# Attention weights' sums in a 128x12 layout for the reciprocal, result copied out ahead of it, value products in three steps a pair

## The chip, the cores and the metric

The kernel runs on one core of one Trainium2 chip. The metric is the time of one execution on the device in microseconds (us), here the median of three runs of the kernel before. A profile is one further execution, recorded by the hardware profiler. The core's engines are TensorE (PE; its weight loads are listed apart as PEld), VectorE (DVE), ScalarE (ACT), GpSimd (POOL) and SyncE (SP), which issues the DMAs. Each engine works through its own list of instructions in order and waits on semaphores for the others. PE writes only to PSUM, from which DVE and ACT read.

## The reference

Two stages: attention in which a query sees only keys of its own cluster, and a mixture of experts on its result.

```python
B, H, S, D = 4, 8, 768, 64          # 16 clusters, 8 experts, DM = 512, DF = 1024
q_assign = argmax(q_n . c_n); k_assign = argmax(k_n . c_n)
mask = q_assign[..., :, None] == k_assign[..., None, :]
scores = where(mask, scale * q @ k.T, -1e9)
scores = scores - scores.max(-1)
attn = exp(scores)
attn = attn / (attn.sum(-1) + 1e-9)
attn_out = attn @ v                              # (B, H, S, D)

x = attn_out.transpose(0, 2, 1, 3).reshape(B * S, H * D)
P = exp(logits - logits.max())                   # logits = x @ w_gate
for _ in range(8): P is normalized by rows, then by columns
for e in range(E):
    out += P[:, e:e+1] * (relu(x @ w1[e]) @ w2[e])
```

A query whose cluster holds no key has the same score everywhere. Its row of attention is then 1/S for every key; the kernel treats such rows by a flag.

## The kernel before, in words

Attention is done in 16 pairs of heads (4 batches of 8 heads). For a pair, q and k are loaded and transposed on PE, split into a high and a low part, and assigned to clusters. For each head, max_chunk (L673) computes scores on PE and takes row maxima on DVE (L688, L692), max_rows (L698) joins them, transposes them and sends them by DMA into rows of the query operand. exp_chunk (L734) computes the scores again, transposed: keys on the partitions, 512 or 256 queries in the free dimension, nine chunks (CHUNKS, L181), each with two products for a tile (L751, L752), and ACT takes the exponential into a tile "pe" (L758), of which there are 14 (PB). The running sum of pe over the blocks of keys goes into a tile "psum" of 128 by 768 in SBUF, on POOL or DVE (L777).

values(p) (L788) multiplies pe with v for both heads of a pair at once: head 0 goes to partitions 0 to 63 of one PSUM tile av_ps (the only one), head 1 to 64 to 127 (L808), chunk by chunk. A small product adds the mean of v for the flagged rows (L816). Then, for 512 and for 256 queries, PE sums psum over its 128 partitions by a product with ones and spreads the sum over the 64 rows of its head (L830); a product with one5 adds the flag and 1e-9 (L831). DVE takes the reciprocal of the whole 128x512 or 128x256 tile (L836) and multiplies av_ps with it into xT (L839). Only then are the tile av_ps and the sums given back, and values of the next pair is started. release (L781) gives a pe tile back once its product and its sum are done.

All of this is a set of Python generators, and nothing of the order is written out by hand: each says on which engine its next step runs and for how long by its own estimate (`yield PE, 0.87, ...`), and a planner (L59) picks steps by start time and by a key (KEYS, L413; urgency, L421: nine units a head). The order that comes out is fixed for every engine. Tokens stand for buffers, so t_v (1) for av_ps, t_x (2) for the two PSUM tiles misc_ps that all small products share, t_pe for the 14 pe tiles. out_batch (L852) writes a batch's xT to memory and computes its logits (L871).

The experts' stage follows. Its weights are loaded and split into fp16 parts (L1020 to L1042), its products are L1110 in the first layer and L1172 to L1174 in the second. Its SBUF tiles lie where those of attention were.

Of the kernel before, what the change touches and what calls it, by code (L numbers as in the profile page):

```python
# [20 lines left out]
P = 128  # L21
# [131 lines left out]
def attn_moe_kernel(  # L153
# [154 lines left out]
    with ExitStack() as actx:  # L308
# [9 lines left out]
        def misc_tile():  # L318
            return ps_x.tile([P, 512], F32, name="misc_ps")
# [55 lines left out]

        mrs = [sm.tile([P, NT, 3], F32, name=f"mrt{i}", bufs=1) for i in range(4)]

        nhs = [sm.tile([5, S], F32R, name=f"nht{i}", bufs=1) for i in range(3)]
# [4 lines left out]
        for t in nhs:  # L383
            nc.vector.memset(t.bitcast(F32), 1.0)
        row5 = sm.tile([5, 1], F32, name="row5", bufs=1)
        nc.gpsimd.iota(row5, pattern=[[0, 1]], base=0, channel_multiplier=1, allow_small_or_imprecise_dtypes=True)
        up2 = sm.tile([5, 1], F32, name="up2", bufs=1)
        nc.vector.tensor_scalar(out=up2, in0=row5, scalar1=2.0, scalar2=None, op0=ALU.is_ge)
        odd = sm.tile([4, 1], F32, name="odd", bufs=1)
        nc.vector.scalar_tensor_tensor(out=odd, in0=up2[0:4], scalar=-2.0, in1=row5[0:4], op0=ALU.mult, op1=ALU.add)  # L390
# [3 lines left out]
        one5 = sm.tile([5, 2, D], F32R, name="one5", bufs=1)  # L394
        tiny = sm.tile([5, 1], F32, name="tiny", bufs=1)
        nc.vector.tensor_scalar(out=tiny, in0=row5, scalar1=4.0, scalar2=1e-9, op0=ALU.is_equal, op1=ALU.mult)
        for x in range(2):
            c_ = sm.tile([5, 1], F32, name=f"of{x}", bufs=1)
            nc.vector.tensor_scalar(out=c_, in0=up2, scalar1=float(x), scalar2=1.0 / S, op0=ALU.is_equal, op1=ALU.mult)
            for g in range(x, G, 2):  # L400
                nc.vector.tensor_copy(halves[:, g], c_[0:4].broadcast_to([4, D]))
            o_ = sm.tile([5, 1], F32, name=f"on{x}", bufs=1)
            nc.vector.scalar_tensor_tensor(out=o_, in0=row5, scalar=2.0 * x, in1=tiny, op0=ALU.is_equal, op1=ALU.add)
            nc.vector.tensor_copy(one5[:, x], o_.broadcast_to([5, D]))

        free = iter([(last[nm, i], f"{nm}{i}") for nm, i in kept])

# [2 lines left out]
        plan = Planner(tc)  # L410
        plan.free.update({PE: 6.0, ACT: 4.0, DVE: 6.3, POOL: 9.0, SP: 2.0})

        KEYS = dict(load=-20, split0=-98.0, split1=-72.5, split2=-33.5, assign=-29.0, place=-30.0, chain=-27.5, ones=-29, max=-18, rows=-38.0, exp=0, values=13.5, out=12.0, batch=27.0, group=-30.0, vsplit=-17.0, vsum=2.5, group0=-18.5, inputs=8, first=1000)  # L413
        NL = 32
        GATES = [0, 0, 1, 0]
        COSTS = [0.66, 0.46, 0.432, 0.214, 0.42]
# [281 lines left out]
        def max_rows(n):  # L698
            for c in range(NCH):
                yield ev["m", n, c]  # L700
            t = heads[n]
            m_, qa = mm[n % 3], t["qa"]
            yield DVE, 0.081
            mr = sm.tile([P, NT], F32, name="mr1")
            nc.vector.tensor_reduce(out=mr, in_=t["mr"], axis=AX, op=ALU.max)
            yield ACT, 0.19
            nc.scalar.copy(m_[:, 0:NT], mr)
            yield POOL, 0.1
            nc.gpsimd.tensor_scalar(out=m_[:, 2 * NT : 3 * NT], in0=mr, scalar1=-BIG / 2, scalar2=None, op0=ALU.is_le)
# [24 lines left out]
        def exp_chunk(n, c):  # L734
# [36 lines left out]
            for part in parts:  # L771
                if a not in old:
                    old[a] = part
                    continue
                n_ = z - a
                e = yield (POOL, 0.06 + n_ * 0.0023), (DVE, 0.08 + n_ * 0.00104, RELUCT[2])
                (nc.gpsimd if e == POOL else nc.vector).tensor_tensor(out=st[:, a:z], in0=old[a], in1=part, op=ALU.add)  # L777
                old[a] = st[:, a:z]
            ev["s", n, c].set(plan)

        def release(p, c):  # L781

            c2 = c + 1 if c == 0 else c
            for x in range(2):
                yield ev["s", 2 * p + x, c2]
                t_pe.put(plan)

        def values(p):  # L788
# [7 lines left out]
            ve = gr["ve"][:, h % G : h % G + 2].rearrange("p h d -> p (h d)")  # L796
            nh = nhs[p % 3]
            av = None
            for c in range(NCH):
                for x in range(2):  # L800
                    yield ev["p", n + x, c]
                yield PE, 0.87, 0.107, 0.43
                if c == 0:
                    av = ps_v.tile([P, 1024], F32, name="av_ps")
                i0, ni, a, z = CHUNKS[c]
                for i in range(i0, i0 + ni):
                    for t, vn, o in two:
                        nc.tensor.matmul(  # L808
                            av[o, a:z], vn[:, i, :], heads[t]["pe", c][:, i - i0], start=(i == 0), stop=False, skip_group_check=True
                        )  # L810
                plan.spawn(release(p, c), plan.now.key)
            for x in range(2):
                yield ev["nh", n + x]
            yield PE, 0.34, 0.107, 0.11
            for a, z in SPANS:
                nc.tensor.matmul(av[:, a:z], ve, nh[0:4, a:z], start=False, stop=True, skip_group_check=True)  # L816
            if h % G == G - 2:
                t_vn.put(plan)
            if h == 0:
                if b:  # L820
                    yield ev["batch", b - 1]
                xts[b] = sm.tile([P, NC, S], F32, name="xT", bufs=1)
            for x in range(2):
                yield ev["s", n + x, NCH - 1]
            for a, z in SPANS:
                yield t_x
                yield PE, (z - a) * 0.0021, 0.107, 0.11
                ps = misc_tile()
                for t, vn, o in two:
                    nc.tensor.matmul(ps[o, 0 : z - a], ones[:, 0:D], heads[t]["sum"][:, a:z], start=True, stop=False, skip_group_check=True)  # L830
                nc.tensor.matmul(  # L831
                    ps[:, 0 : z - a], one5.rearrange("p x d -> p (x d)"), nh[:, a:z], start=False, stop=True, skip_group_check=True
                )
                yield DVE, 0.08 + (z - a) * 0.00104
                ri = work.tile([P, z - a], F32, name="ri", bufs=2)
                nc.vector.reciprocal(ri, ps[:, 0 : z - a])  # L836
                t_x.put(plan)
                yield DVE, 0.08 + (z - a) * 0.00104
                nc.vector.tensor_tensor(out=xts[b][:, h // 2, a:z], in0=av[:, a:z], in1=ri, op=ALU.mult)  # L839
            for x in range(2):  # L840
                t_nh.put(plan)
                t_sum.put(plan)
                ev["v", n + x].set(plan)
            t_v.put(plan)
            if p + 1 < npairs:
                plan.spawn(values(p + 1), urgency("values", 2 * p + 2))
            if h == H - 2:
                plan.spawn(out_batch(b), urgency("batch", n + 1))

# [67 lines left out]
        for n in range(nheads):  # L917
# [389 lines left out]
```

## Time and profile before

| what | us |
|---|---|
| median of three runs | 2567.76 (2566.76 to 2575.36) |
| the profiled execution | 2566.92 |
| its span, first to last instruction | 2565.1 |
| PE busy in the span | 2438.1 |
| DVE busy | 1401.9 |
| ACT busy | 807.5 |
| POOL busy | 674.8 |
| last write of xT (L839) in attention starts at | 609.3 |

A row of a profile group gives the line, the engine, the operation, output and inputs with their shapes, the count, then the busy time in us, the mean time of one in ns, and the engine's idle time just before them with what ended it. A matmul's time in the trace holds its latency, so that two pipelined ones overlap: their rate is read from one start to the next. An fp32 product is recorded as two instructions. PEclk is the share of PE's clock that was granted.

### The profile page before, as it was taken

The numbers are of one execution on the slowest core, as the hardware profiler recorded it, in microseconds if no ns is written. First come the engines' busy times: TensorE is split into PE (matmuls) and PEld (weight loads), VectorE is DVE, ScalarE is ACT, GpSimd is POOL, SyncE is SP. The second block draws the span as 40 slices with busy tenths as digits, with TensorE's granted clock in tenths as the row PEclk, the third lists the DMA queues.
The fourth block names the chain that finished last, engine by engine and source line by source line (L and its number), as shares of the span: only waits on it lengthen the run. The fifth ranks groups of instructions, "written<-read, shape, count | busy, mean of one in ns | idle before, by whom it ended". The sixth has DMA issues, their size and how long they took to land.

```text
span 2565.1 us, 32392 instructions
## 1 busy us (share of the span) xinstructions
PE 2438.1 (95%) x12720; PEld 1281.4 (50%) x12720; DVE 1401.9 (55%) x2349; ACT 807.5 (31%) x1493; POOL 674.8 (26%) x679
## 2 busy tenths in 40 slices
PE   6999999997888999999999999999999999999999
PEld 3455555443444445455545455555555555555554
DVE  7778778686866554444444445644444343443444
ACT  4344444344424242424242422222212222122221
POOL 5667665674424141505050500000000000000000
PEclk7999998999899999999999999999999999999999
DMA  8444434324776554334342422322223223232232
GB/s 179 114 102 110 82 96 103 100 54 146 263 294 236 198 167 137 128 120 158 110 156 99 147 83 85 140 90 97 107 91 112 92 94 110 91 111 93 92 114 93
DMA packets 154681, 320.28 MB, mean 125 GB/s; under 512 B 61088, under 2 KB 90528, under 8 KB 154016
## 3 DMA queue, kind: packets, MB, share of 16 engines
q1 hardware_dynamic: 154528, 318.21, 39.1%
q8 instruction: 100, 1.64, 0.3%
q14 instruction: 53, 0.43, 0.1%
HBM read 230.74 MB, written 58.72 MB: 113 GB/s over the span
## 4 chain that ended last, share of the span: by engine, by line
PE 76%; DVE 9%; POOL 6%; issue 4%; DMA 3%; ACT 1%; SPq 0%; POOLq 0%; ACTq 0%; DVEq 0%
PE h_ps L1110 28%; PE o_ps L1174 11%; PE o_ps L1172 11%; PE o_ps L1173 11%; PE av_ps L808 5%; PE max_ps L688 3%; PE exp_ps L751 3%; DVE ri L836 2%; PE exp_ps L752 2%; POOL r L1030 2%; DMA r<-in_moe_w 2%; DVE mrt L692 2%; POOL wa L1042 2%; DVE am L286 1%; DMA scan<-in_moe_w 1%
## 5 line engine op out<-in xcount | busy, mean ns | idle before, releaser
L1110 PEld LDWEIGHTS <-wa 128*128 128x128 f16 x5376 | 527.6, 98 | 477.4 <-issue 49.8
L1122 DVE SCALAR_TENSOR_TENSOR hl<-c,hh 128x384 f16<-128x384 f32 x512 | 315.4, 616 | 539.9 <-ACT hh L1121 539.4
L1110 PE MATMUL h_ps<-xsT,wa 128*128 128x384 f16 x3072 | 586.0, 327 | 16.1 <-DVE u L1132 10.4
L1174 PE MATMUL o_ps<-wb,hl 128*128 128x512 f16 x1536 | 583.6, 380 | 4.8 <-DVE hl L1122 4.8
L1172 PE MATMUL o_ps<-wb,hh 128*128 128x512 f16 x1536 | 585.0, 381 | 0.0
L1173 PE MATMUL o_ps<-wb,hh 128*128 128x512 f16 x1536 | 584.4, 380 | 0.0
L1121 ACT ACTIVATE hh<-c 128x384 f16<-128x384 f32 x512 | 266.9, 521 | 844.9 <-DVE c L1132 840.5
L1110 PE MATMUL h_ps<-xsB,wa 128*128 128x384 f16 x2304 | 425.4, 329 | 23.1 <-DVE c L1132 14.5
L777 POOL TENSOR_TENSOR psum<-psum,pe 128x512 f32<-128x512 f32 (+1 forms) x237 | 251.5, 1071 | 123.1 <-ACT pe L758 116.4
L758 ACT ACTIVATE pe<-exp_ps 128x512 f32<-128x512 f32 x288 | 168.1, 596 | 267.5 <-PE exp_ps L752 245.9
L1174 PEld LDWEIGHTS <-hl 128*128 128x128 f16 x1536 | 150.6, 98 | 187.4 <-DVE hl L1122 7.3
L1132 DVE SCALAR_TENSOR_TENSOR c<-h_ps,u 128x384 f32<-128x384 f32 x256 | 142.0, 555 | 180.8 <-PE h_ps L1110 179.6
L692 DVE TENSOR_REDUCE mrt<-max_ps 128x1 f32<-128x512 f32 (+1 forms) x288 | 189.8, 680 | 91.9 <-PE max_ps L688 91.0
L1132 DVE SCALAR_TENSOR_TENSOR u<-h_ps,m 128x384 f32<-128x384 f32 x256 | 141.9, 554 | 158.6 <-PE h_ps L1110 158.6
L1172 PEld LDWEIGHTS <-hh 128*128 128x128 f16 x1536 | 151.0, 98 | 141.6 <-issue 2.6
L1173 PEld LDWEIGHTS <-hh 128*128 128x128 f16 x1536 | 151.0, 98 | 140.5 <-issue 2.6
L1137 ACT ACTIVATE c<-h_ps 128x384 f32<-128x384 f32 x128 | 62.5, 489 | 416.6 <-PE h_ps L1110 416.6
L808 PE MATMUL av_ps<-pe,vn 128*64 128x512 f32 (+1 forms) x768 | 153.0, 510 | 8.8 <-DVE xT L839 8.8
L1034 POOL TENSOR_TENSOR wa<-r,wa 128x256 f16<-128x256 f32 (+1 forms) x62 | 58.8, 967 | 389.6 <-ACT wa L1033 389.6
L688 PE MATMUL max_ps<-kX,qX 96*128 96x256 f32 (+1 forms) x384 | 130.3, 408 | 23.1 <-DVE mrt L692 22.6
L1192 DVE SCALAR_TENSOR_TENSOR acc<-o_ps,gates,acc 128x512 f32<-128x512 f32 x168 | 125.3, 746 | 45.7 <-PE o_ps L1174 45.7
L752 PE MATMUL exp_ps<-qX,kX 98*128 98x256 f32 (+1 forms) x384 | 134.5, 361 | 0.0
(187 smaller groups left out, 1966.7 us busy)
## 6 DMA issues: line engine op xcount, KB each, us to landing
wa<-wd SPq DMA_DIRECT2D x96, 896.0 KB
wb<-wd SPq DMA_DIRECT2D x96, 512.0 KB
r<-in_moe_w SPq DMA_DIRECT2D x64, 512.0 KB
wd<-wa SPq DMA_DIRECT2D x32, 896.0 KB
scan<-in_moe_w SPq DMA_DIRECT2D x56, 512.0 KB
wd<-wb SPq DMA_DIRECT2D x32, 512.0 KB
qn<-in_q SPq DMA_DIRECT2D x16, 384.0 KB
kn<-in_k SPq DMA_DIRECT2D x16, 384.0 KB
```

The source lines that it names most:

```text
L688: nc.tensor.matmul(ps[:, y * (z - a) : (y + 1) * (z - a)], t["qa"][0:96, i * P : (i + 1) * P], t["k2"][0:96, a:z], start=True, stop=True)
L692: nc.vector.tensor_reduce(out=t["mr"][:, i0 : i0 + ni, ni - 1], in_=ps.rearrange("p (x c) -> p x c", x=ni), axis=AX, op=ALU.max)
L752: nc.tensor.matmul(o, t["k2"][0:98, ki], t["qa"][0:98, a:z], start=False, stop=True)
L777: (nc.gpsimd if e == POOL else nc.vector).tensor_tensor(out=st[:, a:z], in0=old[a], in1=part, op=ALU.add)
L808: nc.tensor.matmul(av[o, a:z], vn[:, i, :], heads[t]["pe", c][:, i - i0], start=(i == 0), stop=False, skip_group_check=True)
L1110: nc.tensor.matmul(ps[:, 0:HB], wa[:, w_, a, c, :], x[:, x_, c, :], start=(first and s_ == 0), stop=(s_ == len(steps) - 1), skip_group_che ...
L1121: nc.scalar.activation(hh[:, 2 - i, o], src, AF.Relu)
L1122: nc.vector.scalar_tensor_tensor(out=hl[:, 2 - i, o], in0=src, scalar=0.0, in1=hh[:, 2 - i, o], op0=ALU.max, op1=ALU.subtract)
L1132: nc.vector.scalar_tensor_tensor(out=t, in0=ps[:, 0:HB], scalar=KAPPA, in1=x, op0=ALU.mult, op1=ALU.add)
L1172: nc.tensor.matmul(po[i], hh[:, t, ti], wbh[:, t], start=(first and t == 0), stop=False)
L1173: nc.tensor.matmul(po[i], hh[:, t, ti], wbl[:, t], start=False, stop=False)
L1174: nc.tensor.matmul(po[i], hl[:, t, ti], wbh[:, t], start=False, stop=(last and t == 1))
```

## The change

- Value products: a step of values(p) holds three chunks in place of one, so that a pair has three steps.
- values(p) ends with two copies of av_ps to xT on ACT; then av_ps is free and the next pair's values may start.
- A new generator norm(p) takes over the sums. Four products put the sums of a head's halves in four groups of 32 partitions, ACT copies them, three transposes turn them so that queries lie on the partitions, and DVE adds 1e-9 and the flag, takes the reciprocal and splits it into two fp32r parts, on 128x12 values (2 heads of 6 blocks of 128 queries). One transpose brings them to 24x128, ACT copies, and six products with the constant "spread" put each query's reciprocal on its head's 64 rows. DVE multiplies that into xT.
- The flags come from POOL in max_rows in the 128x6 layout, and are no longer taken from the row that a DMA fills; the row of ones in nhs and the constant one5 go.
- Two keys and three planned costs are changed.

```diff
-        KEYS = dict(..., max=-18, ..., vsum=2.5, ...)
+        KEYS = dict(..., max=-27, ..., vsum=-10, ...)
...
+            if n >= 8:
+                yield ev["norm", n // 2 - 4]
+            yield POOL, 0.1
+            o = n % 2 * NT
+            nc.gpsimd.tensor_scalar(out=flags[n // 2 % 4][:, o : o + NT], in0=mr, scalar1=-BIG / 2, scalar2=None, op0=ALU.is_le)
             yield t_x
             yield PE, 0.063, 0.107, 0.06
...
-                e = yield (POOL, 0.06 + n_ * 0.0023), (DVE, 0.08 + n_ * 0.00104, RELUCT[2])
+                e = yield (POOL, 0.33 + n_ * 0.0019), (DVE, 0.1 + n_ * 0.00125, RELUCT[2])
...
-            for c in range(NCH):
-                for x in range(2):
-                    yield ev["p", n + x, c]
-                yield PE, 0.87, 0.107, 0.43
+            for u in range(NCH // 3):
+                for c in range(3 * u, 3 * u + 3):
+                    for x in range(2):
+                        yield ev["p", n + x, c]
+                yield PE, 2.8, 0.107, 0.43
...
+            for a, z in SPANS:
+                yield ACT, 0.15 + (z - a) * 0.00083
+                nc.scalar.copy(xts[b][:, h // 2, a:z], av[:, a:z])
+            t_v.put(plan)
+            ev["raw_x", p].set(plan)
...
-                for t, vn, o in two:
-                    nc.tensor.matmul(ps[o, 0 : z - a], ones[:, 0:D], heads[t]["sum"][:, a:z], start=True, stop=False, skip_group_check=True)
-                nc.tensor.matmul(
-                    ps[:, 0 : z - a], one5.rearrange("p x d -> p (x d)"), nh[:, a:z], start=False, stop=True, skip_group_check=True
-                )
-                yield DVE, 0.08 + (z - a) * 0.00104
-                ri = work.tile([P, z - a], F32, name="ri", bufs=2)
-                nc.vector.reciprocal(ri, ps[:, 0 : z - a])
-                t_x.put(plan)
-                yield DVE, 0.08 + (z - a) * 0.00104
-                nc.vector.tensor_tensor(out=xts[b][:, h // 2, a:z], in0=av[:, a:z], in1=ri, op=ALU.mult)
...
+        def norm(p):
...
+            for g in range(4):
+                nc.tensor.matmul(
+                    ps[g * Q : (g + 1) * Q, 0:HS], ones[:, 0:Q], heads[n + g // 2]["sum"][:, g % 2 * HS : (g % 2 + 1) * HS], start=True, stop=True
+                )
...
+            nc.scalar.copy(sc, ps[:, 0:HS])
...
+            for j in range(NT // 2):
+                nc.tensor.transpose(out=ps2[:, j * P : (j + 1) * P], in_=sc[:, j * P : (j + 1) * P], identity=ident)
...
+            nc.vector.reciprocal(rs, rs)
...
+            nc.tensor.transpose(out=ps.bitcast(F32R)[0 : 2 * R, 0:P], in_=rr.rearrange("p y r -> p (y r)"), identity=ident_r)
...
+            yield ev["raw_x", p]
+            for a, z in SPANS:
...
+                for i in range(a // P, z // P):
+                    nc.tensor.matmul(
+                        ps[:, i * P - a : (i + 1) * P - a], spread[:, i].rearrange("r x d -> r (x d)"), rt, start=True, stop=True
+                    )
+                yield DVE, 0.15 + (z - a) * 0.00104
+                x_ = xts[b][:, h // 2, a:z]
+                nc.vector.tensor_tensor(out=x_, in0=ps[:, 0 : z - a], in1=x_, op=ALU.mult)
...
+        for p in range(npairs):
+            plan.spawn(norm(p), urgency("out", 2 * p + 1))
```

More of the change, by code (lines that the diff above doesn't have):

```diff
@@ L376, in attn_moe_kernel @@
         mrs = [sm.tile([P, NT, 3], F32, name=f"mrt{i}", bufs=1) for i in range(4)]
-        nhs = [sm.tile([5, S], F32R, name=f"nht{i}", bufs=1) for i in range(3)]
+        nhs = [sm.tile([4, S], F32R, name=f"nht{i}", bufs=1) for i in range(3)]
         for t in mm:
@@ L382, in attn_moe_kernel @@
             nc.vector.memset(t, -BIG / 2)
[L383 to L388, printed above, removed]
+        flags = [sm.tile([P, 2 * NT], F32, name=f"flags{i}", bufs=1) for i in range(4)]
+        row4 = sm.tile([4, 1], F32, name="row4", bufs=1)
+        nc.gpsimd.iota(row4, pattern=[[0, 1]], base=0, channel_multiplier=1, allow_small_or_imprecise_dtypes=True)
+        up2 = sm.tile([4, 1], F32, name="up2", bufs=1)
+        nc.vector.tensor_scalar(out=up2, in0=row4, scalar1=2.0, scalar2=None, op0=ALU.is_ge)
         odd = sm.tile([4, 1], F32, name="odd", bufs=1)
-        nc.vector.scalar_tensor_tensor(out=odd, in0=up2[0:4], scalar=-2.0, in1=row5[0:4], op0=ALU.mult, op1=ALU.add)
+        nc.vector.scalar_tensor_tensor(out=odd, in0=up2, scalar=-2.0, in1=row4, op0=ALU.mult, op1=ALU.add)
         sgn4 = sm.tile([4, 1], F32, name="sgn4", bufs=1)
@@ L411, in attn_moe_kernel @@
         plan.free.update({PE: 6.0, ACT: 4.0, DVE: 6.3, POOL: 9.0, SP: 2.0})
-        KEYS = dict(load=-20, split0=-98.0, split1=-72.5, split2=-33.5, assign=-29.0, place=-30.0, chain=-27.5, ones=-29, max=-18, rows=-38.0, exp=0, values=13.5, out=12.0, batch=27.0, group=-30.0, vsplit=-17.0, vsum=2.5, group0=-18.5, inputs=8, first=1000)
+        KEYS = dict(load=-20, split0=-98.0, split1=-72.5, split2=-33.5, assign=-29.0, place=-30.0, chain=-27.5, ones=-29, max=-27, rows=-38.0, exp=0, values=13.5, out=12.0, batch=27.0, group=-30.0, vsplit=-17.0, vsum=-10, group0=-18.5, inputs=8, first=1000)
         NL = 32
@@ L798, in values @@
             av = None
-            for c in range(NCH):
-                for x in range(2):
-                    yield ev["p", n + x, c]
-                yield PE, 0.87, 0.107, 0.43
-                if c == 0:
-                    av = ps_v.tile([P, 1024], F32, name="av_ps")
-                i0, ni, a, z = CHUNKS[c]
-                for i in range(i0, i0 + ni):
-                    for t, vn, o in two:
-                        nc.tensor.matmul(
-                            av[o, a:z], vn[:, i, :], heads[t]["pe", c][:, i - i0], start=(i == 0), stop=False, skip_group_check=True
-                        )
-                plan.spawn(release(p, c), plan.now.key)
+            for u in range(NCH // 3):
[3 more added lines that the diff above has]
+                yield PE, 2.8, 0.107, 0.43
+                if u == 0:
+                    av = ps_v.tile([P, 1024], F32, name="av_ps")
+                for c in range(3 * u, 3 * u + 3):
+                    i0, ni, a, z = CHUNKS[c]
+                    for i in range(i0, i0 + ni):
+                        for t, vn, o in two:
+                            nc.tensor.matmul(
+                                av[o, a:z], vn[:, i, :], heads[t]["pe", c][:, i - i0], start=(i == 0), stop=False, skip_group_check=True
+                            )
+                    plan.spawn(release(p, c), plan.now.key)
             for x in range(2):
                 yield ev["nh", n + x]
-            yield PE, 0.34, 0.107, 0.11
+            yield PE, 0.44, 0.107, 0.11
             for a, z in SPANS:
-                nc.tensor.matmul(av[:, a:z], ve, nh[0:4, a:z], start=False, stop=True, skip_group_check=True)
+                nc.tensor.matmul(av[:, a:z], ve, nh[:, a:z], start=False, stop=True, skip_group_check=True)
             if h % G == G - 2:
                 t_vn.put(plan)
+            for x in range(2):
+                t_nh.put(plan)
+                ev["v", n + x].set(plan)
             if h == 0:
@@ L822, in values @@
                 xts[b] = sm.tile([P, NC, S], F32, name="xT", bufs=1)
+            for a, z in SPANS:
[3 more added lines that the diff above has]
+            ev["raw_x", p].set(plan)
+            if p + 1 < npairs:
+                plan.spawn(values(p + 1), urgency("values", 2 * p + 2))
+        def norm(p):
+            n = 2 * p
+            b, h = divmod(n, H)
             for x in range(2):
@@ L824, in values @@
                 yield ev["s", n + x, NCH - 1]
+            yield t_x
+            yield PE, 0.75, 0.107, 0.64
+            HS = S // 2
+            ps = misc_tile()
+            for g in range(4):
+                nc.tensor.matmul(
+                    ps[g * Q : (g + 1) * Q, 0:HS], ones[:, 0:Q], heads[n + g // 2]["sum"][:, g % 2 * HS : (g % 2 + 1) * HS], start=True, stop=True
+                )
+            for x in range(2):
+                t_sum.put(plan)
+            yield ACT, 0.48
+            sc = work.tile([P, HS], F32, name="sc")
@@ new lines, in norm @@
+            nc.scalar.copy(sc, ps[:, 0:HS])
+            yield PE, 0.36, 0.107, 0.1
+            ps2 = misc_tile()
+            for j in range(NT // 2):
+                nc.tensor.transpose(out=ps2[:, j * P : (j + 1) * P], in_=sc[:, j * P : (j + 1) * P], identity=ident)
+            yield DVE, 0.2
+            rs = work.tile([P, R], F32, name="rs")
+            nc.vector.scalar_tensor_tensor(
+                out=rs.rearrange("p (g j) -> p g j", g=4),
+                in0=ps2[:, 0 : NT // 2 * P].rearrange("p (j g q) -> p g j q", g=4, q=Q)[:, :, :, 0],
+                scalar=1e-9,
+                in1=flags[p % 4].rearrange("p (g j) -> p g j", g=4),
+                op0=ALU.add,
+                op1=ALU.add,
+            )
@@ new lines, in norm @@
+            ev["norm", p].set(plan)
+            t_x.put(plan)
+            yield DVE, 0.2
+            nc.vector.reciprocal(rs, rs)
+            yield DVE, 0.2
+            rr = work.tile([P, 2, R], F32R, name="rr")
+            nc.vector.tensor_copy(rr[:, 0], rs)
+            yield DVE, 0.2
+            nc.vector.tensor_tensor(out=rr[:, 1], in0=rs, in1=rr[:, 0].bitcast(F32), op=ALU.subtract)
+            yield t_x
+            yield PE, 0.065, 0.107, 0.06
+            ps = misc_tile()
+            nc.tensor.transpose(out=ps.bitcast(F32R)[0 : 2 * R, 0:P], in_=rr.rearrange("p y r -> p (y r)"), identity=ident_r)
@@ L825, in values @@
+            yield ACT, 0.25
+            rt = work.tile([2 * R, P], F32R, name="rt")
+            nc.scalar.copy(rt, ps[0 : 2 * R, 0:P])
+            t_x.put(plan)
+            yield ev["raw_x", p]
             for a, z in SPANS:
                 yield t_x
-                yield PE, (z - a) * 0.0021, 0.107, 0.11
+                yield PE, (z - a) / P * 0.06 + 0.1, 0.107, 0.06
                 ps = misc_tile()
-                for t, vn, o in two:
-                    nc.tensor.matmul(ps[o, 0 : z - a], ones[:, 0:D], heads[t]["sum"][:, a:z], start=True, stop=False, skip_group_check=True)
@@ L840, in values @@
[L840 to L846, printed above, removed]
+                for i in range(a // P, z // P):
+                    nc.tensor.matmul(
+                        ps[:, i * P - a : (i + 1) * P - a], spread[:, i].rearrange("r x d -> r (x d)"), rt, start=True, stop=True
+                    )
```

18 lines of the change are left out of this document (8 added, 10 removed).

## The prediction

> What bounds the kernel now.** I read the page first, then the clock and busy times by stage, then the chain of waits of the attention stage, then the timeline around its holes. The page says only that TensorE (PE) is nearly always busy.
>
> ```profile
> PE 2438.1 (95%) x12720; PEld 1281.4 (50%) x12720; DVE 1401.9 (55%) x2349; ACT 807.5 (31%) x1493; POOL 674.8 (26%) x679
> ```
>
> That average covers two stages: attention until about 611 us and the experts after it. All that the change touches lies in the first. Busy time by stage, with the granted clock behind the five engines:
>
> ```profile
> core 0 of [0], span 2565.1 us
> core 0: us, PE busy (x) PEld busy (x) DVE busy (x) ACT busy (x) POOL busy (x), PEclk, DMA share, GB/s
> 48.00:611.00 563.00, 513.46 (x2585) 282.40 (x2586) 424.03 (x611) 245.50 (x483) 365.20 (x396) 0.93 0.40 94
> 113.00:119.00 6.00, 3.43 (x21) 1.44 (x13) 6.00 (x7) 1.66 (x5) 4.71 (x5) 1.00 0.46 135
> 119.00:126.00 7.00, 6.75 (x22) 4.73 (x23) 5.72 (x10) 1.79 (x3) 2.00 (x4) 0.51 1.10 225
> ...
> 577.00:583.00 6.00, 2.50 (x11) 1.38 (x10) 6.00 (x7) 2.17 (x4) 4.01 (x4) 1.00 0.00 0
> 583.00:590.00 7.00, 6.33 (x15) 2.69 (x16) 1.22 (x3) 0.70 (x2) 0.72 (x1) 0.52 0.01 2
> ```
>
> Once attention runs (48 to 611 us) PE is idle for 563.00 - 513.46 = 49.5 us, and its clock averages 0.93, so 563 x 0.07 = 39 us of clock are missing. The losses aren't spread. Stepping through the stage in windows of 1 us I find twelve dips of the clock to half; the first and the last stand above, each with the 6 us ahead of it. There VectorE (DVE) is busy for all 6.00 us while PE stands for 2.57 and 3.50 us; then PE works for about 7 us at 0.51 or 0.52. The chain of waits for the stage names what DVE does then:
>
> ```profile
> by line: PE av_ps L808 22.3%; PE max_ps L688 11.3%; PE exp_ps L751 11.1%; DVE ri L836 9.8%; PE exp_ps L752 8.6%; DVE mrt L692 6.7%; issue 4.3%; PE misc_ps L830 3.5%; PE misc_ps L548 2.5%; POOL psum L777 2.2%; PE misc_ps L584 1.8%; PE misc_p
> ```
>
> L836 is the reciprocal of the spread sums. One of the holes in the timeline (columns: start, length, instruction, idle before it and what ended it):
>
> ```profile
> 400.54 0.40 PE L752 MATMUL exp_ps<-qX,kX 98*128 98x512 f32 x1
> 400.56 1.75 DVE L836 RECIPROCAL ri<-misc_ps 128x256 f32<-128x256 f32 x1
> ...
> 402.82 1.97 PE L808 MATMUL av_ps<-pe,vn 128*64 128x512 f32 x4 [1.89 <-DVE xT L839]
> ```
>
> The next pair's products wait for the one av_ps buffer, which is read by L839, which waits for the reciprocal. The four products then take 1.97 us; at full clock they take 1.08 (below). So what bounds the stage is PE, interrupted about once a pair by DVE.
>
> The change, part by part.** Prices come from these groups (busy us, mean ns, idle ahead) and from PE's timeline.
>
> ```profile
> L836 DVE RECIPROCAL ri<-misc_ps 128x512 f32<-128x512 f32 x16 | 53.7, 3354 | 16.1 <-PE misc_ps L831 16.1
> ...
> L836 DVE RECIPROCAL ri<-misc_ps 128x256 f32<-128x256 f32 x16 | 28.0, 1750 | 5.7 <-PE misc_ps L831 5.7
> ...
> L709 POOL TENSOR_SCALAR mm<-mr 128x6 fp32r<-128x6 f32 x32 | 10.8, 338 | 18.3 <-DVE mr L705 16.2
> ...
> L555 ACT COPY kn<-misc_ps 128x512 f32<-128x512 f32 x16 | 9.4, 586 | 6.0 <-PE misc_ps L548 5.9
> ```
>
> ```profile
> 63.46 1.08 PE L808 MATMUL av_ps<-pe,vn 128*64 128x512 f32 x4
> ...
> 394.32 1.08 PE L830 MATMUL misc_ps<-psum,ones 128*64 128x512 f32 x4
> ...
> 395.75 0.50 PE L751 MATMUL exp_ps<-qH,kL 128*128 128x512 f32 x1
> 396.09 0.40 PE L752 MATMUL exp_ps<-qX,kX 98*128 98x512 f32 x1
> 396.32 0.40 PE L751 MATMUL exp_ps<-qH,kL 128*128 128x512 f32 x1
> ...
> 396.88 0.65 PE L830 MATMUL misc_ps<-psum,ones 128*64 128x256 f32 x4
> ...
> 397.77 0.38 PE L751 MATMUL exp_ps<-qH,kL 128*128 128x256 f32 x1
> ...
> 596.94 0.50 PE L751 MATMUL exp_ps<-qL,kH 128*128 128x512 f32 x1
> 597.28 0.40 PE L752 MATMUL exp_ps<-qX,kX 98*128 98x512 f32 x1
> 597.61 1.08 PE L808 MATMUL av_ps<-pe,vn 128*64 128x512 f32 x4
> 598.62 0.39 PE L751 MATMUL exp_ps<-qL,kH 128*128 128x256 f32 x1
> ...
> 599.30 1.94 PE L808 MATMUL av_ps<-pe,vn 128*64 128x512 f32 x12
> 601.17 0.60 PE L816 MATMUL av_ps<-nht,ve 4*128 4x512 f32 x2
> ```
>
> Part 1, the value products in three steps a pair. I count 115 runs of consecutive L808 products on PE, from 63.46 to 599.30; the new generator issues three chunks back to back, so 16 x 3 = 48 remain, 67 fewer. What does a run cost beside its products? A run of one chunk lasts 597.61 to 598.62 = 1.01 us, one of two chunks 599.30 to 601.17 = 1.87. A chunk is therefore 0.86 and 0.15 is the end of the run. Ahead of a run L752 takes 597.28 to 597.61 = 0.33 us where it otherwise takes 396.09 to 396.32 = 0.23; behind a run the 512-column L751 takes 596.94 to 597.28 = 0.34. That is 0.15 + 0.10 + 0.11 = 0.36 a run, 67 x 0.36 = 24 us of PE time. The chain's line has 61% of the stage on PE in the entries shown, so I count two thirds, 16; bounds 0 and 24.
>
> Part 2, the sums. L830 and L831 held PE from 394.32 to 395.75 and from 396.88 to 397.77, 2.32 us a pair. The new norm(p) streams its four 384-column sums side by side: 384/512 of the 1.01 us, since the two 512-column products of L830 run side by side like a chunk of L808, makes 0.76. Then come three transposes, one transpose of the reciprocals and six products of 128 columns. The nearest rows are the four 256-column products between 598.62 and 599.30, 0.17 each; ten of them make 1.7. Together 2.46 against 2.32: 16 x 0.14 = 2 us lost. If the small ones cost half that it is 11 gained, if each cost 0.33 as ahead of a switch, 28 lost. I take -2, as the 0.17 rows also load new weights for every product.
>
> Part 3, DVE. The reciprocals go: 3.354 + 1.750 = 5.1 us a pair, 82 us in all, and with them the two blocks behind which the max reductions (L692) queue. Two sizes give (3354 - 1750)/256 = 6.3 ns a column and 146 ns fixed, so 12 columns take 0.22 us; add, reciprocal, copy and difference on 12 columns are about 0.9 us, and the two multiplications stay. DVE falls from 424 to about 424 - 16 x 4.2 = 357 us. Idle of PE: the first and last hole are 2.57 and 3.50, twelve at a mean of 3.0 make 36 us. The remaining 13.5 us of PE's idle are spread over all else, and some of the holes will get a successor, as POOL is busy for 365 of 563 us and DVE still for some 60%. I take two thirds, 24; bounds 0 and 36.
>
> Part 4, clock. All twelve dips stand behind a hole that a 3.36 us reciprocal made, and cost 39 us in the stage; PE was busy for 6.75 of 7 us in them, so the time is on the path. Two thirds again: 26; bounds 0 and 39. [...]
>
> Part 5, put at nothing. ScalarE (ACT) gets four copies a pair (both spans of av_ps, the sums, the transposed reciprocals). None is longer than L555's 0.586, so at most 2.3 us a pair, 38 in all; the cover is that ACT is busy for 245.5 of 563 us. Behind such a copy in ACT's queue stand exponentials, for which the next exp_ps product waits; without the cover 38 us would be lost. The copy waits for the last value product, as the reciprocal did, and it frees av_ps sooner. POOL gets one flag operation a head, 32 x 0.338 = 11 us; behind it are the adds of L777, and the idle third of POOL covers it, else 11 are lost. Its new wait, for the norm of four pairs earlier, has long been over. The rows' DMAs on SP come at most 0.34 us later; no DMA is added or moved past another. At the end of the stage the last reciprocals are replaced by a chain of small steps through PE, ACT and DVE; 5.1 us against some ten steps of 0.2 to 0.6, nothing either way (-3 to +2). Keys and planned costs (max earlier by one head, vsum earlier, POOL's adds dearer) only alter the order; -10 to +10, taken as 0, because no row prices an order. The setup swaps small operations for as many.
>
> Sum: 16 - 2 + 24 + 26 = 64 us. The profiled execution took 2566.92 us, its span 2565.1 and 1.8 around it; the median of the runs is 2567.76, 0.8 above, which I leave out. 2566.9 - 64 = **2503**. The end of attention moves from 611 to about 547, and the experts follow unchanged.
>
> Rivals.**
> The holes get other makers. Once the reciprocals are gone PE waits as long for max reductions, for adds on POOL or for ACT's copies. Then parts 3 and 4 give nothing: 16 - 2 = 14, 2553. For it: L692 has 6.7% of the chain by itself. Against: every dip stands behind a reciprocal. 0.14.
> The clock stays. PE's holes shrink, but short ones suffice for a dip, or the cause is another. Then part 4 is lost: 38 gained, 2529. [...] 0.12.
> All of it. Nothing replaces holes, dips and switches: 24 - 2 + 36 + 39 = 97, 2470. For it: PE is nearly without idle between the holes. 0.07.
> Slower: the steps starve. A step takes six of the 14 pe tiles at once, and none comes back before PE's step and POOL's adds on it are through. POOL's instructions average 365.20/396 = 0.92 us. If each of the 48 steps makes PE wait for two of them, 1.85 us, 89 us are lost against 64 gained: 25 slower, 2592. It decides from 64/48 = 1.33 us a step. Against: PE has max products and transposes to fill in with, and POOL has a third of its time free. 0.07.
> Given back. The experts' first products need weights that are loaded and prepared on ACT and DVE at the seam; if that, not attention, sets their start, or if the planner puts the norm so late that values wait for it, the 64 vanish: 2567. Against: attention's buffers lie where these weights go, so the loading moves along. 0.05.
>
> How the numbers follow.** The forecast has 0.55, its own range from 2480 to 2535 (parts 3 and 4 moved by a third, the order by 10). The range over the cases is 2470 to 2553: it takes in the clock rival and ends at the rivals with 97 and 14; left out are slower (0.07), given back (0.05) and about 0.06 beyond the two ends. 0.3% is 7.7 us, about what a measurement here tells from nothing. Faster by more: 0.55 + 0.14 + 0.12 + 0.07 = 0.88; the same 0.05; slower 0.07.
>
> What would show it.** Right: no DVE instruction of 3 us in the chain; the granted clock from 48 us to the end of attention above 0.96; PE's idle there below 30 us; some 48 runs of value products; the last xT near 545 us; the experts' stage as long as before. Wrong: dips of the clock still about once a pair, PE waiting for DVE's mrt or for POOL's psum as long as before, exponentials waiting for pe tiles behind each step, or a seam that grows by what attention lost.

## The result and the profile after

The changed kernel takes 2505.78 us (median of four runs, 2501.97 to 2507.12) against 2569.63 before: a ratio of 0.9746, 95% interval 0.9725 to 0.9768, 64 us less. Its profiled execution took 2501.97, the lowest of its four, with a span of 2500.2.

Busy time by stage in the kernel after (five engines, then the granted clock): attention once it runs, and the only dip of the clock in its middle, with the 7 us ahead of it.

```profile
core 0 of [0], span 2500.2 us
core 0: us, PE busy (x) PEld busy (x) DVE busy (x) ACT busy (x) POOL busy (x), PEclk, DMA share, GB/s
48.00:536.00 488.00, 466.14 (x2712) 281.90 (x2714) 397.96 (x675) 267.33 (x556) 337.85 (x387) 0.99 0.46 108
...
444.00:451.00 7.00, 5.99 (x41) 4.75 (x39) 6.56 (x9) 5.81 (x11) 2.98 (x3) 1.00 0.72 226
451.00:456.00 5.00, 4.08 (x14) 3.34 (x15) 3.76 (x9) 1.71 (x5) 3.24 (x6) 0.66 0.00 0
```

PE's idle in the stage fell from 49.5 us to 21.9, the missing clock from 39 us to some 6 (488 x 0.01 = 5 by the rounded row). The chain of waits for the stage has no reciprocal any more; what DVE still has in it is the max reduction (L693, which was L692):

```profile
by line: PE av_ps L816 20.3%; PE max_ps L689 10.6%; PE exp_ps L757 10.4%; DVE mrt L693 8.7%; PE exp_ps L758 8.5%; issue 3.3%; PE misc_ps L549 2.7%; ACT pe L764 2.2%; PE misc_ps L898 2.1%; PE misc_ps L853 1.8%; DVE vsum L499 1.5%; PE av_ps L
```

One step of the value products and one pass through norm on PE's timeline. The start of the next row gives the price of each: the step 2.73 us, the sums 0.78, the transposes 0.25, four of the spread products 0.59.

```profile
231.01 2.80 PE L816 MATMUL av_ps<-pe,vn 128*64 128x512 f32 x16
233.74 0.73 PE L689 MATMUL max_ps<-kX,qX 96*128 96x256 f32 x3
...
238.66 0.85 PE L853 MATMUL misc_ps<-psum,ones 128*32 128x384 f32 x8
239.44 0.50 PE L689 MATMUL max_ps<-kX,qX 96*128 96x512 f32 x1
...
240.98 0.49 PE L864 MATMUL misc_ps<-ident,sc 128*128 128x128 f32 x3
241.23 0.48 PE L689 MATMUL max_ps<-kX,qX 96*128 96x256 f32 x2
...
246.73 0.66 PE L898 MATMUL misc_ps<-rt,spread 24*128 24x128 f32 x4
247.32 0.50 PE L689 MATMUL max_ps<-kX,qX 96*128 96x256 f32 x2
```

The groups of the new work on DVE (busy us, mean ns):

```profile
L883 DVE TENSOR_TENSOR rr<-rs,rr 128x12 fp32r<-128x12 f32 x16 | 10.7, 669 | 0.1
L881 DVE CAST rr<-rs 128x12 fp32r<-128x12 f32 x16 | 8.6, 537 | 0.1
L878 DVE RECIPROCAL rs<-rs 128x12 f32<-128x12 f32 x16 | 3.4, 215 | 0.1
L867 DVE SCALAR_TENSOR_TENSOR rs<-misc_ps,flags 128x12 f32<-128x12 f32 x16 | 2.6, 162 | 4.1 <-PE misc_ps L864 3.6
```

Attention gained more than the whole kernel. Its last xT starts at 534.3 in place of 609.3, 75 us earlier; what follows took 2500.2 - 534.7 = 1965.5 us in place of 2565.1 - 609.7 = 1955.4, 10 us more. Where that begins can be seen just behind attention: the first rows are PE's (after), the next ACT's (after), the last fence ACT's (before).

```profile
541.83 1.14 PE L1170 MATMUL h_ps<-xsT,wa 128*128 128x384 f16 x6 [0.72 <-DVE u L1192]
548.73 0.37 PE L1021 MATMUL h_ps<-ident,gmax 128*1 128x128 f32 x1 [5.77 <-issue]
```

```profile
541.17 0.48 ACT L1197 ACTIVATE c<-h_ps 128x384 f32<-128x384 f32 x1
543.85 1.04 ACT L1101 CAST wa<-r 128x1024 f16<-128x1024 f32 x1 [2.20 <-POOL r L1090]
544.80 0.52 ACT L1181 ACTIVATE hh<-c 128x384 f16<-128x384 f32 x1
```

```profile
615.85 0.49 ACT L1137 ACTIVATE c<-h_ps 128x384 f32<-128x384 f32 x1 [1.22 <-PE h_ps L1110]
616.43 0.52 ACT L1121 ACTIVATE hh<-c 128x384 f16<-128x384 f32 x1
617.51 1.15 ACT L1020 ACTIVATE r<-r,s 128x1024 f32<-128x1024 f32 x1 [0.55 <-DMA r<-in_moe_w]
```

After, a cast of the next weights (L1101), which waits 2.20 us for POOL, stands in ACT's queue ahead of the first ReLU (L1181), and PE stands for 5.77 us; before, the ReLU came first. The profile shows nothing that ended PE's wait; DVE's rows (after) give the link. L1182 waits for the ReLU, and the maximum "gmax", which PE's next product (L1021) reads, comes behind L1182 in DVE's queue.

```profile
545.42 2.09 DVE L1182 SCALAR_TENSOR_TENSOR hl<-c,hh 128x384 f16<-128x384 f32 x1 [3.65 <-ACT hh L1181]
...
548.30 0.34 DVE L1018 TENSOR_REDUCE gmax<-lg 128x1 f32<-128x192 f32 x1
```

In the 50 us behind the last xT, before and then after, PE is idle for as long, 11.5 and 11.7 us. What differs is the clock, 0.99 against 0.87, which is 6 of the 10 us:

```profile
609.70:659.70 50.00, 38.51 (x200) 18.83 (x199) 41.04 (x80) 27.13 (x40) 28.73 (x24) 0.99 0.76 269
```

```profile
534.70:584.70 50.00, 38.34 (x195) 18.77 (x190) 38.90 (x78) 26.16 (x39) 23.71 (x23) 0.87 0.70 245
```

### The profile page after: what moved, and what is told of

Same layout as the page of the kernel before. It is cut to its first block, busy times and chain, and to the rows that moved or that the text cites. A ratio compares the mean times of both kernels' runs of the same rounds, so it can differ in the third digit from the quotient of the medians.

```text
span 2500.2 us, 32868 instructions
## 1 busy us (share of the span) xinstructions
PE 2397.0 (96%) x12848; PEld 1282.5 (51%) x12848; DVE 1376.1 (55%) x2407; ACT 829.4 (33%) x1565; POOL 647.5 (26%) x671
## 4 chain that ended last, share of the span: by engine, by line
PE 74%; DVE 8%; POOL 7%; DMA 5%; issue 4%; ACT 2%; SPq 0%; POOLq 0%; DVEq 0%; ACTq 0%
PE h_ps L1170 28%; PE o_ps L1232 11%; PE o_ps L1233 11%; PE o_ps L1234 11%; PE av_ps L816 4%; POOL r L1090 2%; PE max_ps L689 2%; PE exp_ps L757 2%; DMA r<-in_moe_w 2%; DVE mrt L693 2%; PE exp_ps L758 2%; DMA scan<-in_moe_w 2%; POOL wa L1102 2%; POOL wb L1099 1%; DVE am L286 1%
## 5 line engine op out<-in xcount | busy, mean ns | idle before, releaser
L1182 DVE SCALAR_TENSOR_TENSOR hl<-c,hh 128x384 f16<-128x384 f32 x512 | 316.6, 619 | 534.4 <-ACT hh L1181 534.1
L1181 ACT ACTIVATE hh<-c 128x384 f16<-128x384 f32 x512 | 267.0, 522 | 860.2 <-DVE c L1192 856.4
L783 POOL TENSOR_TENSOR psum<-psum,pe 128x512 f32<-128x512 f32 (+1 forms) x216 | 232.4, 1093 | 57.7 <-ACT pe L764 50.2
L693 DVE TENSOR_REDUCE mrt<-max_ps 128x1 f32<-128x512 f32 (+1 forms) x288 | 190.5, 681 | 26.0 <-PE max_ps L689 23.8
L816 PE MATMUL av_ps<-pe,vn 128*64 128x512 f32 (+1 forms) x768 | 134.4, 492 | 0.0
L1090 POOL TENSOR_TENSOR r<-r 128x256 f32<-128x256 f32 x124 | 100.0, 827 | 126.0 <-ACT r L1080 123.9
```

Of the source, the lines that this page charges most:

```text
L693: nc.vector.tensor_reduce(out=t["mr"][:, i0 : i0 + ni, ni - 1], in_=ps.rearrange("p (x c) -> p x c", x=ni), axis=AX, op=ALU.max)
L816: nc.tensor.matmul(av[o, a:z], vn[:, i, :], heads[t]["pe", c][:, i - i0], start=(i == 0), stop=False, skip_group_check=True)
L1181: nc.scalar.activation(hh[:, 2 - i, o], src, AF.Relu)
L1182: nc.vector.scalar_tensor_tensor(out=hl[:, 2 - i, o], in0=src, scalar=0.0, in1=hh[:, 2 - i, o], op0=ALU.max, op1=ALU.subtract)
```

## The experiments

Theory A: the long reciprocals on DVE make the holes of PE, and the holes the dips of the clock. Theory B: what counts is that av_ps is held until the result is multiplied. Theory C: what counts is the order, that is steps, keys and planned costs. All runs were timed against the kernel before on the same chip, whose median was 2568.25 to 2571.77 there; differences between two medians of the table hold to some us only. "Idle" and "clock" are PE's, from 48 us to the end of attention in the profiled run, "dips" the falls of the clock that begin between 60 us and the last xT, "rest" the span behind that xT.

| kernel | median us | ratio to before (95%) | idle us | clock | dips | rest us |
|---|---|---|---|---|---|---|
| before | | | 49.5 | 0.93 | 12 | 1955.4 |
| after | 2505.78 | 0.9746 (0.9725 to 0.9768) | 21.9 | 0.99 | 2 | 1965.5 |
| e1, constant for reciprocal | 2502.74 | 0.9741 (0.9726 to 0.9757) | 12.0 | 1.00 | 0 | 1960.1 |
| e2, three steps only | 2555.71 | 0.9949 (0.9931 to 0.9968) | 49.4 | 0.91 | 11 | 1959.8 |
| e3, after, nine steps | 2514.15 | 0.9786 (0.9769 to 0.9803) | 14.7 | 0.98 | 2 | 1966.2 |
| e4, after, reciprocals put back | 2559.74 | 0.9964 (0.9951 to 0.9976) | 56.5 | 0.93 | 12 | 1970.4 |
| e5, after, old keys and costs | 2509.58 | 0.9766 (0.9748 to 0.9785) | 23.6 | 0.98 | 4 | 1966.9 |
| e6, copy out only | 2567.75 | 0.9998 (0.9988 to 1.0007) | 43.6 | 0.92 | 15 | 1959.9 |
| e7, true cost planned | 2532.09 | 0.9850 (0.9829 to 0.9872) | 28.6 | 0.96 | 6 | 1961.6 |
| e9, e1 and three steps | 2491.37 | 0.9699 (0.9681 to 0.9717) | 20.0 | 1.00 | 1 | 1959.7 |
| e10, exp(-ln) on ACT | 2551.50 | 0.9937 (0.9914 to 0.9959) | 48.5 | 0.95 | 11 | 1958.8 |
| e11, e4 with its cost planned | 2529.46 | 0.9843 (0.9825 to 0.9860) | 26.5 | 0.96 | 6 | 1968.4 |
| e12, after, four true costs | 2504.51 | 0.9751 (0.9732 to 0.9769) | 20.4 | 0.98 | 4 | 1967.7 |
| e14, e7 and three steps | 2529.98 | 0.9846 (0.9824 to 0.9868) | 35.9 | 0.96 | 7 | 1955.5 |

**Take away only the length of the reciprocals.**

```diff
-                nc.vector.reciprocal(ri, ps[:, 0 : z - a])
+                nc.vector.tensor_scalar(out=ri, in0=ps[:, 0 : z - a], scalar1=4.3e-4, scalar2=None, op0=ALU.mult)
```

> The kernel before, with both wide reciprocals (L836) replaced by a multiplication with a constant of the same shape, so that the weights are not normalized; planned costs and the order of attention are those of before. Theory A (the long reciprocals on DVE make the holes of PE and, behind them, the dips of the clock): at most 3 dips after 48 us, PE's idle in the stage from 49.5 to about 25 us, 2505 to 2535. Theory B (what counts is that av_ps is held until the result is multiplied): the hold shrinks here from some 7 us to 3 but stays, dips remain at about half, 2540 to 2555. Theory C (what counts is the order: three steps, keys, planned costs): the order is unchanged, 2555 to 2572.

2502.74 us: 66 us less, with nothing else touched; PE's order in attention is instruction for instruction that of before. That is A, and a little beyond its range. The stage in e1, and what PE still waits for in it (but for one wait of 0.5 us):

```profile
48.00:539.00 491.00, 478.99 (x2579) 263.44 (x2580) 366.98 (x610) 240.74 (x480) 368.36 (x396) 1.00 0.45 107
```

```profile
PE misc_ps L714 <- POOL mm L710: 5.8, 7, 1.4
PE max_ps L688 <- DVE mrt L692: 3.3, 10, 0.8
PE exp_ps L751 <- ACT pe L758: 0.8, 3, 0.3
PE av_ps L808 <- DVE xT L839: 0.8, 1, 0.8
```

The columns are the sum in us, the number and the longest. Before, the same two waits for DVE were 22.6 and 8.8 us (20 to 611 us):

```profile
PE max_ps L688 <- DVE mrt L692: 22.6, 18, 2.8
PE av_ps L808 <- DVE xT L839: 8.8, 5, 3.9
```

**Put only the length back.** In norm, ahead of each last multiplication:

```diff
+                for y in range(0, z - a, HS):
+                    w = min(HS, z - a - y)
+                    nc.vector.reciprocal(sc[:, 0:w], ps[:, y : y + w])
                 x_ = xts[b][:, h // 2, a:z]
```

> The changed kernel, with dead reciprocals of 512 and 256 columns (three instructions, the result unused) put on DVE ahead of the two last multiplications of norm; they are not in the planned costs, so the order of attention is that of the changed kernel. A: some 5.3 us of DVE a pair come back, with them holes of 2 to 4 us and a dip of the clock behind most of them: 2545 to 2575. B: av_ps is free early all the same, 2505 to 2520. C: the order is that of the changed kernel, 2505 to 2520.

2559.74: nearly all of the gain is gone, although av_ps is copied out first and the order is that of the changed kernel. One of its twelve dips, in the profiled run, which is the longest of its ten (2566.7); the median is 7 us below it.

```profile
395.48 0.50 PE L689 MATMUL max_ps<-kX,qX 96*128 96x256 f32 x2 [1.05 <-DVE mrt L693]
...
395.94 3.53 DVE L904 RECIPROCAL sc<-misc_ps 128x384 f32<-128x384 f32 x2
...
399.39 0.63 DVE L906 TENSOR_TENSOR xT<-misc_ps,xT 128x512 f32<-128x512 f32 x1
399.94 0.68 DVE L693 TENSOR_REDUCE mrt<-max_ps 128x2 f32<-128x512 f32 x1
400.17 0.66 PE L898 MATMUL misc_ps<-rt,spread 24*128 24x128 f32 x2 [2.23 <-DVE xT L906]
```

```profile
389.00:396.00 7.00, 5.95 (x36) 3.64 (x36) 7.00 (x13) 2.05 (x4) 6.05 (x6) 1.00 0.95 194
396.00:407.00 11.00, 8.77 (x28) 3.30 (x27) 9.80 (x14) 2.27 (x5) 3.54 (x7) 0.53 0.15 33
```

```profile
395.40:396.70 1.30, 1.23 (x8) 1.02 (x8) 1.30 (x3) 0.20 (x1) 0.74 (x2) 1.00 0.92 201
396.90:398.00 1.10, 1.04 (x3) 0.09 (x2) 1.10 (x1) 0.78 (x2) 0.73 (x1) 0.50 0.58 123
```

PE waits 1.05 us for a max reduction, and the clock falls to half at 396.7. From 397.94 PE waits another 2.23 us for a tile that DVE has not read; that wait lies within the dip, which ends at 407.

**Only the copy out, only the three steps.** e6 moves two ACT copies of av_ps and the start of the next values ahead of the sums:

```diff
+            for a, z in SPANS:
+                yield ACT, 0.15 + (z - a) * 0.00083
+                nc.scalar.copy(xts[b][:, h // 2, a:z], av[:, a:z])
+            t_v.put(plan)
+            if p + 1 < npairs:
+                plan.spawn(values(p + 1), urgency("values", 2 * p + 2))
...
-                nc.vector.tensor_tensor(out=xts[b][:, h // 2, a:z], in0=av[:, a:z], in1=ri, op=ALU.mult)
+                x_ = xts[b][:, h // 2, a:z]
+                nc.vector.tensor_tensor(out=x_, in0=x_, in1=ri, op=ALU.mult)
```

> The kernel before, with only av_ps copied to xT on ACT ahead of the sums; the wide reciprocals stay and multiply xT. A: the waits of PE for av_ps (8.8 us in the profile before) go, but the max reductions still queue behind 3.36 us and 1.75 us, so that most dips stay: 2550 to 2575. B: 2505 to 2530. C: a new order without a better cost, 2555 to 2575.

e2 takes the loop of the change's first part, with the products in it unchanged:

```diff
-            for c in range(NCH):
-                for x in range(2):
-                    yield ev["p", n + x, c]
-                yield PE, 0.87, 0.107, 0.43
+            for u in range(NCH // 3):
+                for c in range(3 * u, 3 * u + 3):
+                    for x in range(2):
+                        yield ev["p", n + x, c]
+                yield PE, 2.8, 0.107, 0.43
```

> The kernel before, with only the value products in three steps a pair. A: 48 runs in place of 115 save 16 to 24 us of PE time, while reciprocals, holes and dips stay as they are: 2545 to 2560. B: the same or less, 2550 to 2570. C, with the three steps as the cause: 2505 to 2530. If steps of six pe tiles starve the exponentials: above 2575.

2567.75 for the copy: nothing, and 15 dips (the profiled run, 2574.11, is again the longest of its ten). PE no longer waits for av_ps, so B falls. 2555.71 for the steps: 12.6 us, somewhat under the 16 expected, with idle and dips as before.

**The steps and the keys in the changed kernel.** e3 takes that last diff back in the kernel after.

> The changed kernel with the value products in nine steps a pair, as before. If the three steps give here what they gave alone (2568.3 to 2555.7, 12.6 us): 2514 to 2524. If they only filled holes that are gone now: 2502 to 2510. If they starve the exponentials: below 2500.

e5 gives `max`, `vsum` and the step of the running sums their old numbers:

```diff
-max=-27, ... vsum=-10
+max=-18, ... vsum=2.5
-                e = yield (POOL, 0.33 + n_ * 0.0019), (DVE, 0.1 + n_ * 0.00125, RELUCT[2])
+                e = yield (POOL, 0.06 + n_ * 0.0023), (DVE, 0.08 + n_ * 0.00104, RELUCT[2])
```

> The changed kernel with the two keys and the planned cost of the running sums as before. Theory A (the time is the length of the reciprocals): 2500 to 2514. Theory C (part of the gain is the keys and costs): 2520 to 2545.

e9 is the kernel before with the edits of e1 and of e2.

> The kernel before with the reciprocals replaced by a multiplication with a constant (the weights are not normalized) and with three steps a pair. If the two gains add (65.6 and 12.6 us): 2486 to 2495, and the difference to the changed kernel, some 15 us, is what the way through 128x12 costs. If the three steps only filled holes: 2499 to 2506, and that way costs little.

The steps are worth 8.4 us there (2514.15 against 2505.78) and 11.4 on e1 (2502.74 against 2491.37): they add to the rest, less than alone. Keys and planned costs of the sums are worth 4 us at most, inside A's range; the two sets of runs overlap (2505.66 to 2512.37 against 2501.97 to 2507.12). e9 stands 14 us below the changed kernel: so much dearer is the way through 128x12, with its rest, than a spread whose reciprocal costs no more than a multiplication. Of the 12 us between the two profiled runs 6 lie in attention and 6 behind it.

**Is it the length, or that the plan didn't know it?** The planner counted the reciprocal of 512 columns at 0.08 + 512 x 0.00104 = 0.61 us; it takes 3.354.

```diff
-                yield DVE, 0.08 + (z - a) * 0.00104
+                yield DVE, 0.15 + (z - a) * 0.0063
                 ri = work.tile([P, z - a], F32, name="ri", bufs=2)
```

> The kernel before, with the planned cost of the two reciprocals set to what they take (0.15 us and 6.3 ns a column in place of 0.08 us and 1.04 ns), nothing else. Theory A: DVE is still blocked for 3.36 us at a time and a plan can only hide part of it: 2545 to 2568. Theory C (a plan that believes in 0.61 us makes the holes, not the reciprocal itself): 2505 to 2530.

2532.09: 36 us less by one number in the plan, with every reciprocal still there. This is between the two ranges, and nearer to C: A as stated is too simple: how long the reciprocals are matters most where the plan doesn't know it. The stage in e7 and its longest waits of PE:

```profile
48.00:570.00 522.00, 493.39 (x2591) 276.21 (x2585) 423.36 (x598) 251.94 (x493) 370.50 (x402) 0.96 0.44 101
```

```profile
PE misc_ps L548 <- DVE ri L836: 6.6, 4, 2.6
PE max_ps L688 <- DVE mrt L692: 4.3, 5, 1.6
```

DVE is as busy as before, 423 us, but PE waits for its max reductions for 4.3 us in place of 22.6, since in the new order PE has other things to do while DVE divides. The counterpart is e4 with its dead reciprocals entered in the plan:

```diff
-                yield DVE, 0.15 + (z - a) * 0.00104
+                yield DVE, 0.5 + (z - a) * 0.0073
```

> The changed kernel with the dead reciprocals of 512 and 256 columns in norm, as in the run that put them back, but now with their time in the planned cost of the step (0.5 us and 7.3 ns a column). If the unplanned length is the larger part of the harm, as the run with true costs in the kernel before says (36 of 65 us): 2515 to 2538, against 2559.7 unplanned. If DVE's time itself is what counts: 2545 to 2565.

2529.46 against 2559.74 unplanned, 30 us: near the 36 of e7, from the other side. e14 is e7 with the loop of e2.

> The kernel before with the reciprocals' true time in the plan and the value products in three steps a pair; sums, spread and wide reciprocals as before. If the two gains add (36.2 and 8 to 13 us): 2518 to 2526, and the way through 128x12 with the copy is worth the remaining 12 to 20 us. If the longer steps undo what the plan hides: 2530 to 2550. If that way adds nothing to a right plan: 2500 to 2510.

2529.98: on a right plan the three steps add 2 us, which the runs can't tell from nothing. So the gains don't add; PE's idle is 35.9 us in place of e7's 28.6. The new way of the sums with the copy, and with the keys that e5 priced at 4 us at most, keeps 24 us (2529.98 to 2505.78).

**Two tries for something better.** e12 enters four measured means in the plan of the kernel after (max reduction, two steps of POOL, exp):

```diff
-            yield DVE, 0.598
+            yield DVE, 0.68
...
-            yield POOL, 0.1
+            yield POOL, 0.58
...
-            yield POOL, 0.1
+            yield POOL, 0.34
...
-            yield ACT, 0.5
+            yield ACT, 0.597
```

> The changed kernel with four more planned costs set to what the profile shows: max reduction 0.68 us, exponential 0.597, POOL's pair of operations in max_rows 0.58, flags 0.34. If plans that are off by 0.1 to 0.5 us a step cost time in proportion to the reciprocals' 4.1 us a pair: 2485 to 2500. If errors below the slack of the buffers cost nothing: 2500 to 2510.

e10 is e2 with the reciprocal as exp(-ln) on ACT:

```diff
-                yield DVE, 0.08 + (z - a) * 0.00104
-                nc.vector.reciprocal(ri, ps[:, 0 : z - a])
+                yield ACT, 0.15 + (z - a) * 0.00083
+                nc.scalar.activation(ri, ps[:, 0 : z - a], AF.Ln)
+                yield ACT, 0.15 + (z - a) * 0.00083
+                nc.scalar.activation(ri, ri, AF.Exp, scale=-1.0)
```

> The kernel before with three steps a pair and the reciprocal of the spread sums made on ACT as exp(-ln(sum)), two instructions for each span, planned at their length. If Ln and Exp need no reload of tables between them, ACT has some 2 us a pair more and DVE 5.1 less, without the way through 128x12: 2488 to 2503. If every change of function reloads a table (1.28 us in the profile before) some four times a pair: 2560 to 2600.

2504.51 for e12 can't be told from the 2505.78 of the change: errors of 0.1 to 0.5 us a step cost nothing that could be measured. e10 gets 2551.50, only 4 us below e2, and ACT reloads its tables:

```profile
L838 ACT ACT_TABLE_LOAD  x32: 1283/1283/1283, 79.9 to 584.0; - x32
L841 ACT ACT_TABLE_LOAD  x17: 1283/1283/1283, 117.7 to 585.7; - x17
L758 ACT ACT_TABLE_LOAD  x16: 1283/1283/1283, 47.3 to 559.6; - x16
```

These are 65 loads, four a pair, 83 us of ACT; the price was the one named, the harm smaller than forecast. That the reloads hold e10 back, and that part of them fell on ACT's idle time, is argued: no run leaves them out. No version that computes the whole reference beats the changed kernel by more than can be measured.

## Why the prediction was right, and where not

The time was 2503 forecast and 2505.8 measured, but by two errors that cancel: attention ended at 534.7, not at 547, and the experts took 10 us more, not the same. That the two nearly cancel is luck.

Parts 3 and 4, holes and clock, carry the result as forecast. Forecast were 24 us of idle and 26 of clock, measured 28 and 33; 14 of the 75 us are left for parts 1 and 2, where 14 were forecast. Two thirds was too careful, as nothing of that size took the place of the holes. The 36 us that it was taken of were too many, though: PE's waits ahead of the twelve dips sum to 29 us, 2.4 each, and the row of 577 to 583 us belongs to the eleventh dip, not the last. Two of the twelve holes, this one and the one shown that ends at 402.82, stand at the reciprocal of 256 columns, not at the 3.36 us one. e1 shows that taking away the length of the two reciprocals is enough for all of it, e4 that putting it back undoes nearly all. The rivals that kept holes or clock are out, and so is the one in which the steps starve (e2 and e9 gain by them).

What the prediction didn't see is why 82 us of DVE did such harm on an engine with a quarter of its time free. It had the planned cost of the step, 0.61 us, in the listing beside the 3.354 us of the profile, and never set the one against the other. e7 and e11 show that 30 to 36 us of the loss come from that difference. It also put "an order" at nothing for want of a row; e7's order alone was worth 36 us.

Part 1: the 48 runs came out exactly, at 2.73 us each. Worth 16 forecast, 12.6 alone, 8.4 in the changed kernel, at most 2 on a right plan. There PE's idle grew by 7 us: PE time that is saved counts only where PE is what bounds.

Part 2: 2.46 us a pair forecast for the new sums on PE. Measured are 0.78, 0.25 and 0.59 in the rows above, 0.07 for the last transpose and 0.36 for the other two spread products: 2.05, less than the 2.32 removed. The small products were mis-sized; at 16 x 0.27 = 4 us gained in place of 2 lost it matters little.

Part 3's figure for DVE, 357 us, was wrong: it is 398. L881 and L883 took 537 and 669 ns where 220 were counted, and the plan handed DVE more of the running sums, 41 adds in place of 22.

Part 5, the end of attention at nothing and the experts unchanged, failed. In the eight kernels without norm, "rest" is 1955 to 1962 us, in the six with norm 1965 to 1970, whatever their order within attention: on average 9 us go with norm. The rows show a wait of ACT for POOL ahead of the first ReLU, 5.77 us of idle PE in one piece and a lower clock behind it; why the instructions of the seam come in that order with norm was not tested and stays open. "Given back" was thus a rival of the whole gain, and came true for a seventh.

The rival in which the clock stays had its condition half right. Short holes did suffice for a dip: in the kernel before the clock fell at 402.3, when 1.4 us of the 1.89 us wait were over, and in e4 behind a wait of 1.05 us. But few such holes were left, and the clock rose from 0.93 to 0.99.

## What to carry to other kernels

Where the order is fixed by a plan, set every planned cost against the mean in the profile first: an error of 4 us a pair on an engine that looked a quarter free cost 30 to 36 us here, one of 0.1 to 0.5 us a step cost nothing that could be measured. A long instruction on an engine that others wait for cost more than the waits here: the holes it tore into PE were paid a second time, as half clock for 3.4 to 10.2 us each in the kernel before. And a small layout for an operation that is slow per column (reciprocal: 3354 ns on 512 columns, 215 on 12) pays even with ten small steps around it, though they aren't free: e9, which leaves the normalization out, is 14 us faster, an estimate of what is still to be had.

## What the runs showed of the hardware that was not expected

**Small operations of DVE beside POOL.** In the changed kernel two operations of DVE on 12 columns from SBUF to SBUF (L881, L883) took 537 and 669 ns on average, where the one that reads PSUM (L867) took 162. At the end of attention, with no POOL instruction beside them, both took 0.17 us:

```profile
531.34 0.17 DVE L867 SCALAR_TENSOR_TENSOR rs<-misc_ps,flags 128x12 f32<-128x12 f32 x1 [3.02 <-PE misc_ps L864]
531.54 0.23 DVE L878 RECIPROCAL rs<-rs 128x12 f32<-128x12 f32 x1
531.80 0.17 DVE L881 CAST rr<-rs 128x12 fp32r<-128x12 f32 x1
532.01 0.17 DVE L883 TENSOR_TENSOR rr<-rs,rr 128x12 fp32r<-128x12 f32 x1
```

In the trace of the changed kernel the long ones end with an instruction of POOL. Beside an idle POOL the cast took 0.16 us; the difference took 1.13 and ended at 216.87, 0.03 us behind an instruction of POOL that had started ahead of it:

```profile
214.81 0.16 DVE L881 CAST rr<-rs 128x12 fp32r<-128x12 f32 x1
...
215.57 1.27 POOL L783 TENSOR_TENSOR psum<-psum,pe 128x512 f32<-128x512 f32 x1 [1.15 <-ACT pe L764]
...
215.74 1.13 DVE L883 TENSOR_TENSOR rr<-rs,rr 128x12 fp32r<-128x12 f32 x1
```

Of the 32 instructions of the two lines 25 took 280 ns or more, and each of these ended 28 to 34 ns behind an instruction of POOL; the other seven took 161 to 174. The reciprocal, from SBUF too, took 204 to 228 ns, in 15 of its 16 instructions with one of POOL beside it.

**Where the clock fell.** In the kernel before, the twelve dips begin at 119.0, 153.2, 190.7, 262.4, 334.1, 368.2, 402.3, 436.5, 474.0, 545.7, 583.3 and 607.1 us, whole multiples of 3.413 us apart, and last 3.41, 6.83 or 10.24 us, one, two or three times that. The same holds in each of the other thirteen profiles for all dips from 60 us on, by windows of 1 us; e2, e4 and e6 have one of 13.6 to 13.7 us, four times 3.41. With the time cut into steps of 3.41 us at these points, the step ahead of each dip of the kernel before holds 1.57 to 3.41 us of idle PE, in one wait or several, and no step from 55 us on that was followed by full clock holds more than 1.36. In the kernel after, the steps ahead of its two dips hold 1.84 and 1.78 us, and none followed by full clock more than 1.09. Over attention from 50 us on in all fourteen, every step at full clock with 1.8 us or more of idle PE was followed by a half one and none with less than 0.68 (e5, e11); in between both occur, up to 1.73 us ahead of full clock (e14). So a step that is partly idle was enough. The length of a wait alone did not decide: in e4 PE was idle for 3.14 us between 330 and 334 us, 1.7 us of it in one step and 1.5 in the next, and no dip followed.
